# Instruction order of every engine from a list scheduler at build time, in a channel attention and highway network kernel

## The chip, the cores and the metric

The kernel runs on one core of a Trainium2 chip. The metric is the device time of one execution in microseconds (us). Every run that is quoted was taken as fast (undisturbed). A profiled run's span, from its first to its last instruction, is about 1.8 us shorter than its time (349.39 against 347.5 us, 307.13 against 305.3 us). Runs of one call share a chip and the runs of the kernel before; different calls ran on different chips, so across calls I compare ratios or stretches of a profile.

## The reference

There are four batches of N = 6336 tokens with C = 256 channels. The attention is over channels: the score matrix is only 256 x 256 per batch, but it is a sum over all tokens. A gated layer follows.

```python
qn = q / (np.linalg.norm(q, axis=1, keepdims=True) + 1e-06)   # over the tokens
kn = k / (np.linalg.norm(k, axis=1, keepdims=True) + 1e-06)
s = kn.transpose(0, 2, 1) @ qn / tau                          # 256 x 256 for each batch
a = softmax(s)                                                # over the last axis
x = v @ a
H = relu(x @ w_h);  T = sigmoid(x @ w_t + b_t)
out = T * H + (1 - T) * x
```

## The kernel before

Each batch has three parts, and they depend on each other in this order.

- **Stage 1**: 50 steps of six matmuls on TensorE (PE) that sum k·q and the two Gram matrices, whose diagonals are the squared norms, in one accumulator `sg`.
- **The chain**: from `sg` to the attention matrix. VectorE (DVE) takes the diagonals and computes roots and reciprocals in some 20 tiny operations, each needing the one before; PE spreads the result over the partitions (`cqb`); then come scale, exp on ScalarE (ACT), row sums, four transposes on PE (`atps`) and a fold with the layer's weights (`ah`). Almost nothing of it is work; it is latency.
- **Stage 2**: 25 pairs of row blocks (100 in the whole program). For each, PE transposes v (`vtps`), multiplies (`xh`) and computes the gate (`t`); ACT does a relu and the gate's function; DVE does a difference and, for every second pair, a product and the result.

Stage 2 of a batch is mixed with stage 1 of the next. The order was written by hand: `due` tells how many stage-1 steps should be done after a pair, and one step of the chain is taken after each pair. Every engine executes in the order in which instructions are written: the timeline in the prediction shows PE standing 5.79 us before `cqb`, with the next pair written behind it.

```python
LOOK = 2
ENDS = [17, 42, 69]          # the pairs at which stage 1 of batches 1, 2, 3 ends
...
    def chain(b):
        ...
        first = [diagonals, guess, refine, root, bcast]        # bcast holds the matmul cqb
        if b == B - 1:
            return [lambda: [f() for f in first], exps, soft, trans, fold]
        return [diagonals, lambda: (guess(), refine()), lambda: (root(), bcast()),
                exps, soft, trans, fold]
...
        if end:                                                # the last batch
            eng = nc.gpsimd if i % 4 == 1 and not single else nc.vector
            eng.tensor_tensor(out=dd[...], in0=uu[...], in1=dd[...], op=AluOp.mult)
...
            xh, tt = main(b, i)                                # PE: the pair
            got = elementwise(b, i, xh, tt, pending)           # ACT and DVE
            ...
            want = due(g)
            if steps:
                steps.pop(0)()                                 # one step of the chain
            while s1 < want:                                   # stage-1 steps of the next batch
                stage1(1 + s1 // NS, s1 % NS)
                s1 += 1
                if s1 % NS == 0:
                    steps = chain(s1 // NS)
                    steps.pop(0)()
```

## Time and profile before

| | before |
|---|---|
| time, median of 3 runs | 349.55 us (349.28 to 349.7) |
| span of the profiled run | 347.5 us |
| PE busy | 288.6 us, 83% |
| DVE, ACT, GpSimd busy | 59%, 51%, 18% |
| mean granted PE clock | 0.944 |

The page's rows of busy tenths cut the span into 40 slices; a nine means 90% or more. The view that I use most, though, is the start of each pair's `xh` matmuls in the timeline. A pair costs PE 1.74 us and a stage-1 step 0.44; where two pairs start further apart than the work between them, PE has stood still or run at half clock. The prediction shows the slices, the stretches and the timeline.

### The profile page before, as it was taken

Reading aid. Unit: us, or ns where it says so; the run is one execution under the profiler, and the core shown is the slowest. Engines: PE = TensorE matmul, PEld = TensorE weight load, DVE = VectorE, ACT = ScalarE, POOL = GpSimd, SP = SyncE. Lnnn points to the kernel's source line nnn. Section 1 sums busy time; section 2 is a strip of 40 time slices with the busy share of each in tenths; the row PEclk is TensorE's granted clock in tenths of the full one; section 3 lists DMA queues with packets and bytes.
Section 4 is the critical chain, followed back from the end, with each engine's and each line's share of the span. In section 5 each row is a group of like instructions: output and inputs, shape, how many; then the busy total and the mean of one; then the engine's idle time right before and its main releaser. Section 6 shows DMA issues by size and latency. Waiting matters only on the chain.

```text
span 347.5 us, 6183 instructions
## 1 busy us (share of the span) xinstructions
PE 288.6 (83%) x2540; PEld 207.1 (60%) x2540; DVE 206.0 (59%) x331; ACT 177.8 (51%) x322; POOL 63.1 (18%) x102
## 2 busy tenths in 40 slices
PE   0969699999995789999995789999993786888883
PEld 0858567777773467777763467776772354555541
DVE  1000235666675377677686277777677385777775
ACT  1000246666561355665672365666662378777762
POOL 6214422212111212211111000000010002222220
PEclk9998989999998799999999799999997699999995
DMA  7999999999999999999999963466643203222233
GB/s 132 213 213 211 209 214 213 222 265 271 269 245 244 234 251 247 248 270 271 250 252 258 232 146 143 75 170 181 173 144 61 121 1 145 121 121 123 121 124 143
DMA packets 16828, 65.54 MB, mean 189 GB/s; under 512 B 1952, under 2 KB 3616, under 8 KB 13856
## 3 DMA queue, kind: packets, MB, share of 16 engines
q0 software_dynamic: 12608, 39.20, 58.1%
q1 hardware_dynamic: 4192, 25.95, 18.6%
q8 instruction: 20, 0.33, 0.3%
q14 instruction: 8, 0.07, 0.1%
HBM read 78.38 MB, written 25.95 MB: 300 GB/s over the span
## 4 chain that ended last, share of the span: by engine, by line
PE 56%; DVE 17%; DMA 8%; issue 6%; ACT 5%; POOL 4%; POOLq 1%; ACTq 0%; DVEq 0%
PE xh L398 19%; PE sg L191 9%; PE t L408 8%; DVE o L473 6%; PE vtps L381 5%; DMA q<-in_q_dram 5%; PE sg L193 5%; PE sg L192 5%; DVE dd L438 4%; PE t L405 4%; POOL dd L449 3%; DMA k<-in_k_dram 3%; ACT hh L431 3%; DVE dd L453 1%; DVE junk L213 1%
## 5 line engine op out<-in xcount | busy, mean ns | idle before, releaser
L438 DVE TENSOR_TENSOR dd<-hh,xh 128x512 f32<-128x512 f32 (+1 forms) x100 | 68.7, 687 | 81.5 <-ACT hh L431 80.9
L431 ACT ACTIVATE hh<-xh 128x512 f32<-128x512 f32 (+1 forms) x100 | 59.7, 597 | 100.3 <-PE xh L398 57.1
L398 PE MATMUL xh<-mr,vtsb 128*128 128x512 f16 (+1 forms) x400 | 108.0, 394 | 2.0 <-DVE vtsb L386 2.0
L191 PE MATMUL sg<-q,k 128*128 128x256 f16 x384 | 95.4, 286 | 14.3 <-DMA k<-in_k_dram 13.3
L193 PE MATMUL sg<-q 128*128 128x128 f16 x384 | 87.4, 228 | 0.0
L192 PE MATMUL sg<-k 128*128 128x128 f16 x384 | 87.4, 227 | 0.0
L432 ACT ACTIVATE uu<-t 128x512 f32<-128x512 f32 (+1 forms) x100 | 59.7, 597 | 7.7 <-PE t L408 2.2
L473 DVE SCALAR_TENSOR_TENSOR o<-dd,hh 128x1024 f32<-128x1024 f32 (+1 forms) x49 | 58.7, 1198 | 4.9 <-POOL dd L449 4.9
L408 PE MATMUL t<-mr,vtsb 128*128 128x256 f16 (+1 forms) x400 | 61.2, 276 | 0.0
L384 ACT COPY vtsb<-vtps 128x512 f16<-128x512 f16 (+1 forms) x93 | 53.6, 577 | 13.3 <-PE vtps L381 13.3
L408 PEld LDWEIGHTS <-vtsb 128*128 128x128 f16 (+1 forms) x400 | 40.3, 101 | 29.1 <-issue 4.6
L398 PEld LDWEIGHTS <-vtsb 128*128 128x128 f16 (+1 forms) x400 | 36.7, 102 | 28.3 <-issue 3.8
L381 PE MATMUL vtps<-ident,v 128*128 128x128 f16 x384 | 37.5, 221 | 15.3 <-DVE gs L294 7.4
L453 DVE SCALAR_TENSOR_TENSOR dd<-uu,dd 128x1024 f32<-128x1024 f32 (+1 forms) x39 | 46.2, 1184 | 4.4 <-ACT uu L432 0.9
L191 PEld LDWEIGHTS <-k 128*128 128x128 f16 x384 | 39.3, 102 | 15.5 <-DMA k<-in_k_dram 13.8
L193 PEld LDWEIGHTS <-q 128*128 128x128 f16 x384 | 39.4, 103 | 6.1
L381 PEld LDWEIGHTS <-v 128*128 128x128 f16 x384 | 29.8, 99 | 19.3 <-issue 17.0
L405 PE MATMUL t<-btb,row 128*128 128x512 f16 (+1 forms) x100 | 39.0, 390 | 1.7 <-ACT uu L432 1.7
L192 PEld LDWEIGHTS <-k 128*128 128x128 f16 x384 | 39.4, 103 | 0.9 <-issue 0.5
L80 POOL DMA_DIRECT2D v<-in_v_dram x24 | 12.8, 533 | 109.0 <-PE vtps L381 71.6
L213 DVE SCALAR_TENSOR_TENSOR junk<-sg,ident 128x128 f32<-128x128 f32 x16 | 4.6, 290 | 36.1 <-ACT gs L209 35.7
L449 POOL TENSOR_TENSOR dd<-uu,dd 128x1024 f32<-128x1024 f32 x6 | 14.2, 2361 | 65.1 <-DVE dd L438 65.1
(63 smaller groups left out, 130.6 us busy)
## 6 DMA issues: line engine op xcount, KB each, us to landing
out_dram<-o SPq DMA_DIRECT2D x23, 1024.0 KB, 4.6
v<-in_v_dram POOLq DMA_DIRECT2D x24, 512.0 KB, 19.2
q<-in_q_dram POOLq DMA_DIRECT2D x23, 512.0 KB, 20.2
k<-in_k_dram POOLq DMA_DIRECT2D x23, 512.0 KB, 20.2
out_dram<-ot SPq DMA_DIRECT2D x4, 192.0 KB, 2.6
q<-in_q_dram POOLq DMA_DIRECT2D x2, 256.0 KB, 14.5
k<-in_k_dram POOLq DMA_DIRECT2D x2, 256.0 KB, 11.2
out_dram<-o SPq DMA_DIRECT2D x1, 512.0 KB, 2.7
```

The lines of the kernel that those rows point to most:

```text
L191: nc.tensor.matmul(sg[:, c, 0:C], ka[:, cs], qa, start=first, stop=False)
L192: nc.tensor.matmul(sg[:, c, C : C + P], ka[:, cs], ka[:, cs], start=False, stop=False)
L193: nc.tensor.matmul(sg[:, c, C + P : C + 2 * P], qa[:, cs], qa[:, cs], start=False, stop=last)
L381: nc.tensor.transpose(ps[:, u, c, 0:nr], src[:, bass.ts(c, P)], ident[0:nr, 0:nr])
L384: eng.copy(out=vt[:, :, :, 0:nr], in_=ps[:, :, :, 0:nr])
L398: nc.tensor.matmul(xh[0:nr, u, :], vt[:, u, kt, 0:nr], mr[kt][:, 0 : 2 * C], start=(kt == 0), stop=(kt == 1),)
L405: nc.tensor.matmul(tt[0:nr, :, :], row0[:, 0:nr], btb, start=True, stop=False)
L408: nc.tensor.matmul(tt[0:nr, u, :], vt[:, u, kt, 0:nr], mr[kt][:, 2 * C : 3 * C], start=False, stop=(kt == 1 and u == 0),)
L431: nc.scalar.activation(out=hh[0:nr, us, :], in_=xh[0:nr, :, C : 2 * C], func=Act.Relu)
L432: nc.scalar.activation(out=uu[0:nr, us, :], in_=tt[0:nr, :, :], func=Act.Sigmoid if end else Act.Tanh, scale=-1.0 if end else -0.5,)
L438: nc.vector.tensor_tensor(out=dd[0:nr, us, :], in0=hh[0:nr, us, :], in1=xh[0:nr, :, 0:C], op=AluOp.subtract)
L473: nc.vector.scalar_tensor_tensor(out=ot, in0=dd[0:nr, us, :], scalar=-1.0 if end else -0.5, in1=hh[0:nr, us, :], op0=AluOp.mult, op1=AluOp ...
```

## The change

All arithmetic becomes tasks. A task knows its engine, a key (smaller is sooner), how long it occupies the engine (`pitch`), how long until its result can be used (`lat`), what it depends on, and which buffers it takes and frees. At build time a simulation picks, whenever an engine is free, the ready task with the smallest key. Loads and stores run through a model of the DMA (a common rate, a lag, at most eight loads under way). The simulated order is then emitted as the program. The chain's tasks have key -50, so they go before everything that is ready.

```diff
-LOOK = 2
-ENDS = [17, 42, 69]
+ENDS = [16, 41, 68]
+class Plan:
+    RATE = 422e3
+    LAG = 1.8
+    LANES = 8
...
+        def ready(x):
+            return (
+                not x.left
+                and x.at <= t + eps
+                and all(self.rings[g].open_at(t + eps) for g in x.take)
+                and (x.eng != "POOL" or not x.size or sum(d > t + eps for d in lanes) < self.LANES)
+            )
...
+            return min(
+                (x for x in avail[e] if ready(x)), key=lambda x: (x.key, x.n), default=None
+            )
...
+        def several(fns, x):                   # a row of tiny DVE operations as one task
+            d = 0.2 * len(fns)
+            return dve(lambda: [f() for f in fns], d - 0.06, d, [x])
...
+        cqb = x = pe(bcast, 0.85, [x], take=["vt"])
...
+        ready[b] = plan_chain(b, first, x, -50)
...
+            xh[i] = plan.add(
+                "PE", g, 0.86, 1.06, [ev[i]] + ready[b], lambda i=i: main_xh(b, i), take=["xh"]
+            )
...
-            if steps:
-                steps.pop(0)()
-            while s1 < want:
-                stage1(1 + s1 // NS, s1 % NS)
...
-            eng = nc.gpsimd if i % 4 == 1 and not single else nc.vector
...
+    nc.scalar.preload_act_table(Act.Sqrt)
+    for x in plan.run():
+        if x.fn is not None:
+            x.fn()
```

Besides the order, some things change in kind: the last batch uses tanh like the others and no longer gives every fourth product to GpSimd; all copies of transposed v go to ACT; several copies of the chain move from DVE to ACT in batches 1 to 3; and in batch 0 the table for the root is loaded at the start, that for exp directly after the root.

## The prediction

> **What bounds the kernel now.** I read the busy table of the page first (PE 288.6 us, 83% of the span; DVE 59%; ACT 51%), then the slices, then busy time by stretches of 20 us. A share over the whole span hides that there are several stages, so the stretches decide. First PE's row of the slices, in tenths:
>
> ```profile
> PE   0969699999995789999995789999993786888883
> ```
>
> Then the stretches. Columns: stretch; its length; busy us of PE, PEld, DVE, ACT, POOL; granted clock; DMA share; GB/s.
>
> ```profile
> 20.00:40.00 20.00, 16.26 (x195) 14.61 (x192) 0.26 (x2) 0.86 (x2) 6.21 (x11) 0.91 1.10 209
> ...
> 80.00:100.00 20.00, 20.00 (x200) 15.15 (x199) 13.24 (x15) 12.09 (x23) 3.71 (x7) 1.00 1.06 264
> 100.00:120.00 20.00, 12.98 (x93) 8.44 (x91) 11.64 (x35) 7.58 (x16) 4.23 (x8) 0.86 1.06 240
> ...
> 180.00:200.00 20.00, 12.71 (x82) 8.28 (x81) 10.81 (x34) 6.68 (x14) 1.58 (x3) 0.83 1.06 249
> ...
> 240.00:260.00 20.00, 20.00 (x193) 14.83 (x192) 14.40 (x17) 13.23 (x24) 1.57 (x3) 1.00 0.56 155
> 260.00:280.00 20.00, 11.70 (x66) 6.70 (x64) 11.25 (x36) 7.44 (x17) 0.00 (x0) 0.74 0.31 84
> ...
> 300.00:320.00 20.00, 17.16 (x126) 10.62 (x125) 14.06 (x18) 14.91 (x27) 7.09 (x3) 1.00 0.38 155
> ```
>
> The reader is to see four stages. Until 39 us PE waits for q and k of batch 0 (DMA full). From 51 us PE is full, with three holes near 110, 190 and 270 us: there the softmax chains of batches 1 to 3 run. From 285 us, when no q, k work (stage 1) is left, PE is no longer full.
>
> Next I took the start of each of the 100 row pairs (the groups of four L398 matmuls in the timeline). In the full stretches the spacing is 2.62 us with two stage-1 steps between, 2.18 with one, 3.06 with three, 1.74 with none: so a pair costs PE 1.74 us and a step 0.44, without exception. Every spacing above that is lost time:
> - chain 1, pairs 18 to 23: 29.2 us where 6 x 2.62 = 15.7 are due. 13.5 over, of which the chain's own matmuls are 1.9 (0.85 + 0.22 + 0.86). Lost: 11.6.
> - chain 2, pairs 43 to 48: 28.9 against 15.3. Lost: 11.7.
> - chain 3, pairs 69 to 73: 24.2 against 9.6. Lost: 12.7.
> - last stage: pairs 76, 78, 82, 86, 90, 94 take 3.3 to 3.6 each instead of 1.74. Lost: 9.9. Pair 98 takes 3.71: lost 2.0.
>
> Sum 47.9 us of the 347.5 us span. The timeline shows why for chain 3:
>
> ```profile
> 262.63 0.59 ACT L209 COPY gs<-sg 128x512 f32<-128x512 f32 x1
> 263.44 0.28 DVE L213 SCALAR_TENSOR_TENSOR junk<-sg,ident 128x128 f32<-128x128 f32 x1
> ...
> 268.39 1.19 PE L288 MATMUL cqb<-dcat,ones 128*128 128x256 f32 x2 [5.79 <-DVE dcat L279]
> ...
> 269.37 1.91 PE L398 MATMUL xh<-mr,vtsb 128*128 128x512 f16 x4
> ...
> 271.37 0.60 ACT L431 ACTIVATE hh<-xh 128x512 f32<-128x512 f32 x1 [8.15 <-PE xh L398]
> ```
>
> The order written by hand puts the broadcast matmul cqb right behind the last stage-1 step. PE is in order, so it stands 5.8 us while VectorE does some 20 tiny dependent operations (about 0.2 us each, 0.16 busy), and the next pair then runs at half clock. In the last stage the idle of PE is due to one thing in each four pairs: a product given to GpSimd, on which VectorE and then PE wait; it takes 2361 ns there, and the same product takes 1225 ns on VectorE (groups by form):
>
> ```profile
> L453 DVE SCALAR_TENSOR_TENSOR dd<-uu,dd 128x1024 f32<-128x1024 f32 x36 | 44.1, 1225 | 4.4 <-ACT uu L432 0.9
> ...
> L449 POOL TENSOR_TENSOR dd<-uu,dd 128x1024 f32<-128x1024 f32 x6 | 14.2, 2361 | 65.1 <-DVE dd L438 65.1
> ```
>
> **What the Trainium skill says.** "TensorE: Matmul & The Clock Gate", part 1 (What's actually happening), says the array falls to half clock after about 3.4 us of idleness and needs about 3.4 us of work to return. The trace agrees: after the holes four matmuls of 512 take 1.91 us instead of 1.03, and a stage-1 step 0.85 instead of 0.44 from 42.96 to 45.94 us; a hole of 2.2 us (ending at 24.85 us) was enough too. So a hidden hole gives back its length and some 1.7 us more (half of 3.4; an estimate). "ScalarE: Activation LUTs", What ACT_TABLE_LOAD costs, gives about 1283 ns for a table load; the page here has four of 1283 ns, and § Table sets puts exp and tanh in one set, which the trace confirms (no load between them). "Perfetto Trace Analysis", Optimizing Scalar/DVE Operations, says that profiled latency exceeds engine time because the write's end overlaps with the next instruction. The trace agrees: 128x512 on VectorE lasts 0.69 but the next starts 0.60 later; 128x1024 lasts 1.22 and gives way after 1.14; ACT 0.60 against 0.50.
>
> **The change part by part.** The arithmetic is nearly the same: 5070 rows on PE in both programs. I read the changed program's order on each engine.
>
> 1. Chains 1 and 2. Between the last stage-1 step and cqb, PE now has 2 pairs less a little, 2 transposes and 6 steps of the next batch: 2 x 0.86 + 2 x 0.64 + 2 to 3 x 0.22 + 6 x 0.44 = 6.2 us. VectorE needs for the same: 4 diagonals 1.34, one 0.60 difference, 17 small ones 3.4, and a wait of up to 1.14 for a running operation: about 6. From cqb to the transposes of the softmax, PE has 4.5 us (2 pairs' products, 3 steps) against scale 0.75 behind up to 2.3 of VectorE work, exp 1.3, reciprocal 0.35, two scalings 0.7: some 5. I allow 1.5 us of loss per chain: gain 10.1 + 10.2.
>
> 2. Chain 3 has no next batch to fill with. Up to cqb PE has 3 xh (2.58), 2 t (1.28) and 5 transposes (1.1): 5.0 us, but the 2 buffers of xh make pairs 70 and 71 wait for differences that stand in VectorE's order behind the diagonals and behind the small ones. Walking the order by hand, the first pair of batch 3 starts some 17 to 18 us after the last step, with about 12.5 us of PE work in it. I take 5.5 us lost: gain 7.2.
>
> 3. Chain 0. The sqrt table is loaded at the start and the exp table behind the root; the copy of sg moves behind the diagonals. The chain's inputs come 0.6 (copy) and 1.28 (table) earlier. But PE's order now has all 8 steps and a transpose before the softmax transposes, and after 2.8 us of idleness they would run at half clock: 4 x 0.85 + 4 x 0.44 + 0.2 = 5.4 us after cqb, about the time of before (8 of before's were also there). Gain 0.5, at most 2.
>
> 4. Last stage, 25 pairs. GpSimd's 6 products of 2.36 return to VectorE, sigmoid becomes tanh (one table load of 1.28 less, at 288 us). VectorE per two pairs: 2 x 0.60 + 2 x 1.14 = 3.48, plus about 0.12 where the product waits for the difference just before it, so 1.80 a pair; PE needs 1.74; ACT 3 x 0.50. The stage is thus bound by VectorE and PE almost equally. Gain 9.9 less 25 x 0.08 = 2: 7.9.
>
> 5. The end. The copy of the last transposed pair goes back to ACT without waiting: of 2.0 us I count 1.5 and 1.0 for the last pair, now at full clock. Gain 2.5.
>
> Sum 0.5 + 10.1 + 10.2 + 7.2 + 7.9 + 2.5 = 38.4. Span 347.5 - 38.4 = 309.1; the timed runs are 2.05 above the span (349.55), so **311 us**.
>
> **Rivals.** (a) The transfers become the bound. For: the DMA share is above 1 until 200 us. A load of 1.05 MB is issued every 2.46 us, 426 GB/s. "DMA: Bandwidth & Descriptors", Where 436 GB/s comes from, gives about 435 as the ceiling, so there is no more to be had. Against: up to the end of stage 1 of batch 1 some 35 such units (q, k of two batches 25, v 6, outputs 4) are due, 3 + 86 = 89 us, and PE is there at 97 at best; for batch 3 it is about 213 against some 238. The margin is 8 us in the first phase, and late tiles would cost there: time 316 to 322. (b) The static order is wrong on the chip: a scheduler that takes a wait for 0.5 us too short puts an instruction in front that blocks an in-order engine. For: chain 3's cqb stands behind pair 71. Every chain losing 4 us more would give 323. (c) VectorE bounds more than the last stage, because it took over GpSimd's work; at 1.95 a pair the stage gains 4 us less: 315. (d) All chains hide completely, also chain 3: 311 - 3 - 4 = 304.
>
> **Range and chances.** Costs I can't see are likelier than gains: 304 to 321. To lose the 2% (7 us), four fifths of the gain would have to vanish, though 48 us of idle PE are really there: faster 0.97, within 2% 0.02, slower 0.01.
>
> **What would show it.** Spacing of pairs near 18 to 24 and 43 to 49 close to 1.74 + 0.44 per step; no idle of PE before cqb above 1.5 us for chains 1 and 2; clock 1.0 in those stretches; stage 1 of batch 3 over near 238 us; a spacing of 1.8 in the last stage and VectorE 95% busy there; PE waits for DMA only before 39 us. New DMA waits at 50 to 100 us, or half clock in the chains, would make it wrong.

## More of the kernel before

One more view of the kernel before: PE's waits, by what it waited for. Columns: total us, number of waits, longest.

```profile
PE cqb L288 <- DVE dcat L279: 17.4, 4, 5.8
PE sg L191 <- DMA k<-in_k_dram: 13.3, 4, 9.2
PE vtps L381 <- DVE gs L294: 7.4, 3, 2.6
PE vtps L381 <- DVE vtsb L386: 7.2, 5, 1.5
```

The reader is to see that the first and third row are the chain, at two different places; the fourth is the last stage, where PE waits for a copy of transposed v on DVE. The second is the start, in which PE waits for the first q and k.

## The result and the profile after

| | before | after |
|---|---|---|
| time, median of 4 runs | 349.41 us (346.51 to 349.7) | 307.86 us (307.13 to 308.78) |
| span of the profiled run | 347.5 us | 305.3 us |
| PE busy | 288.6 us, 83% | 274.8 us, 90% |
| DVE busy | 206.0 us, 59% | 204.6 us, 67% |
| mean granted PE clock | 0.944 | 0.996 |

The ratio is 0.883 (95% interval 0.877 to 0.888). A ratio here is the mean time of one kernel's fast runs over the mean of the other's fast runs of the same rounds, so not quite the ratio of the medians. The output is correct in this and in every run below.

PE's slices and clock in the page after, in tenths:

```profile
PE   0886867999999999999999999999999789999981
...
PEclk9999999999999999999999999999999999999998
```

Of the three holes one shallow dip is left, and the last quarter is full. The stretches of the kernel after (columns as in the prediction):

```profile
100.00:120.00 20.00, 20.00 (x193) 15.04 (x192) 16.65 (x34) 13.85 (x29) 3.69 (x7) 1.00 1.05 264
160.00:180.00 20.00, 19.56 (x178) 13.96 (x176) 17.73 (x45) 13.79 (x29) 3.69 (x7) 1.00 1.06 254
...
240.00:260.00 20.00, 16.67 (x118) 10.20 (x116) 18.31 (x32) 15.94 (x33) 0.00 (x0) 1.00 0.29 116
260.00:280.00 20.00, 19.98 (x149) 12.41 (x147) 19.37 (x23) 17.83 (x35) 0.00 (x0) 1.00 0.29 119
280.00:300.00 20.00, 17.50 (x120) 10.25 (x118) 19.44 (x24) 15.12 (x29) 0.00 (x0) 1.00 0.46 185
```

The first two stretches hold chains 1 and 2: PE is full, where before it had 12.98 of 20 us near 110. The third holds chain 3. The last two are the last stage: DVE is 97% busy and PE keeps up with it until the work runs out near 299 us. PE's waits of the kernel after:

```profile
PE sg L354 <- DMA k<-in_k_dram: 13.9, 5, 8.9
PE cqb L512 <- DVE dcat L500: 2.6, 1, 2.6
PE t L653 <- ACT uu L684: 2.5, 2, 1.3
PE xh L641 <- ACT mr L601: 1.6, 2, 1.2
```

The wait at `cqb` has become one of 2.6 us instead of four with 17.4; it is chain 0's, for which there is no stage 2 to fill with. The DMA wait is the start, as before; after 45 us PE waits for no DMA at all. By the starts of the pairs, the span divides like this (us; "lost" is what exceeds the PE work between those pairs at full clock, with the chain's own matmuls taken as work):

| part | before | after | gain |
|---|---|---|---|
| start to the first pair | 50.87 | 49.38 | 1.5 |
| chain 1, lost | 11.6 | 0.15 | 11.5 |
| chain 2, lost | 11.7 | 0.6 | 11.1 |
| chain 3, lost | 12.7 | 4.8 | 7.9 |
| last stage (pairs 75 to 98), lost | 9.9 | 1.2 | 8.7 |
| from pair 98 to the end | 11.9 | 11.3 | 0.6 |
| the chains' own matmuls, now at full clock | 3 x 1.93 | 3 x 1.57 | 1.1 |

The gains sum to 42.4 us, and the spans differ by 42.2. As an example of the working: after the change pairs 18 to 24 start within 20.47 us after pair 17; seven pairs at 1.74, 15 steps at 0.4375 and 1.57 us of chain matmuls make 20.31, so 0.15 us are lost.

### The profile page after: what moved, and what is told of

Read it like the earlier page. It is cut to its first block, busy times and chain, and to the rows that moved or that the text cites. A ratio compares the mean times of both kernels' runs of the same rounds, so it can differ in the third digit from the quotient of the medians.

```text
span 305.3 us, 6171 instructions
## 1 busy us (share of the span) xinstructions
PE 274.8 (90%) x2540; PEld 200.0 (66%) x2540; DVE 204.6 (67%) x321; ACT 178.5 (58%) x336; POOL 48.7 (16%) x96
## 4 chain that ended last, share of the span: by engine, by line
PE 63%; DVE 18%; DMA 9%; issue 3%; ACT 3%; POOL 1%; ACTq 0%; DVEq 0%; POOLq 0%
PE xh L641 20%; PE sg L354 11%; PE t L656 10%; PE sg L355 6%; PE sg L356 6%; DMA q<-in_q_dram 6%; DVE o L722 6%; DVE dd L693 5%; PE vtps L628 5%; PE t L653 5%; DVE dd L703 5%; DMA k<-in_k_dram 4%; PE ah L590 1%; DVE junk L391 1%; ACT hh L676 1%
## 5 line engine op out<-in xcount | busy, mean ns | idle before, releaser
L354 PE MATMUL sg<-q,k 128*128 128x256 f16 x384 | 93.0, 276 | 14.6 <-DMA k<-in_k_dram 13.9
L641 PE MATMUL xh<-mr,vtsb 128*128 128x512 f16 (+1 forms) x400 | 102.7, 379 | 2.7 <-ACT mr L601 1.6
L355 PE MATMUL sg<-k 128*128 128x128 f16 x384 | 85.1, 222 | 0.0
L356 PE MATMUL sg<-q 128*128 128x128 f16 x384 | 85.1, 222 | 0.0
L703 DVE SCALAR_TENSOR_TENSOR dd<-uu,dd 128x1024 f32<-128x1024 f32 (+2 forms) x53 | 61.6, 1163 | 14.3 <-ACT uu L684 12.9
L656 PE MATMUL t<-mr,vtsb 128*128 128x256 f16 (+1 forms) x400 | 60.0, 273 | 0.0
L634 ACT COPY vtsb<-vtps 128x512 f16<-128x512 f16 (+1 forms) x100 | 57.7, 577 | 2.3 <-PE vtps L628 2.2
L354 PEld LDWEIGHTS <-k 128*128 128x128 f16 x384 | 38.0, 99 | 21.2 <-DMA k<-in_k_dram 14.6
L355 PEld LDWEIGHTS <-k 128*128 128x128 f16 x384 | 38.1, 99 | 7.7 <-issue 1.1
L356 PEld LDWEIGHTS <-q 128*128 128x128 f16 x384 | 38.0, 99 | 4.8
L653 PE MATMUL t<-btb,row 128*128 128x512 f16 (+1 forms) x100 | 37.9, 379 | 2.5 <-ACT uu L684 2.5
## 6 DMA issues: line engine op xcount, KB each, us to landing
q<-in_q_dram POOLq DMA_DIRECT2D x2, 256.0 KB, 14.6
k<-in_k_dram POOLq DMA_DIRECT2D x2, 256.0 KB, 11.3
```

The lines of the kernel that those rows point to most:

```text
L354: nc.tensor.matmul(sg[:, c, 0:C], ka[:, cs], qa, start=first, stop=False)
L355: nc.tensor.matmul(sg[:, c, C : C + P], ka[:, cs], ka[:, cs], start=False, stop=False)
L356: nc.tensor.matmul(sg[:, c, C + P : C + 2 * P], qa[:, cs], qa[:, cs], start=False, stop=last)
L634: nc.scalar.copy(out=vt[:, :, :, 0:nr], in_=vt_ps.pop((b, i))[:, :, :, 0:nr])
L641: nc.tensor.matmul(xh[0:nr, u, :], vt[:, u, kt, 0:nr], mr[kt][:, 0 : 2 * C], start=(kt == 0), stop=(kt == 1),)
L656: nc.tensor.matmul(tt[0:nr, u, :], vt[:, u, kt, 0:nr], mr[kt][:, 2 * C : 3 * C], start=False, stop=(kt == 1 and u == 0),)
```

## The experiments

My theory: the gain is that of PE's idle time, in two independent pieces. Each chain is a row of waits on an engine that executes in order, and the scheduler puts other PE work between its steps; in the last stage PE no longer waits for DVE, which stood behind GpSimd. Four rivals:

- **One instruction**: a single badly placed one per chain (`cqb`) causes the whole loss, and no scheduler is needed.
- **Urgency** makes the gain.
- **Transfers** are the next bound, and the DMA model is what keeps the order right.
- **Any scheduler** would do; its durations need not be precise.

Where an expectation names theories by letters, the letters belong to that text alone. In the timeline lines below, the columns are the start, the duration, engine, line and operation, output and inputs, and in brackets the idle time before it and what ended that.

### The last stage alone (on the kernel before)

```diff
-            func=Act.Sigmoid if end else Act.Tanh,
-            scale=-1.0 if end else -0.5,
+            func=Act.Tanh,
+            scale=-0.5,
...
-            eng = nc.gpsimd if i % 4 == 1 and not single else nc.vector
...
-                on_dve = b == B - 1 and i % 4 == 2
-                transposes(n // NP, n % NP, nc.vector if on_dve else nc.scalar)
+                transposes(n // NP, n % NP, nc.scalar)
```

> The kernel before, with only the last batch changed as the new kernel has it: products on VectorE instead of GpSimd, tanh instead of sigmoid, all transposed pairs copied by ACT. My theory: the GpSimd product is what makes pairs 76 to 94 take 3.3 us each now and then, so the last stage gains about 8 us and the three chains stay as they are: 341 us (339 to 343), spacing 1.74 to 1.85 us in the last stage. Rival (the GpSimd product is not the cause, the hand-made order is): under 3 us gained, 346 to 349.

Measured: 340.81 us (338.16 to 341.54) against 349.25, ratio 0.976 (0.970 to 0.981): a gain clear of noise, though not surely one of 2%. The chains still lose 12.4, 11.7 and 12.4 us, and pairs from 77 on are 1.74 us apart, later 1.74 and 1.92 in turn. The stretch of this kernel that lies wholly in the last stage:

```profile
300.00:320.00 20.00, 19.93 (x146) 12.34 (x145) 19.48 (x23) 18.59 (x35) 0.00 (x0) 1.00 0.34 138
```

PE went from 17.16 (as the prediction shows it) to 19.93 of 20 us, with the same DVE rate as in the scheduled kernel. So 8.4 us of the 42 have nothing to do with the scheduler: moving six products from GpSimd to DVE, the gate and the copies by hand gives them. The edit makes these three changes at once, and no run takes them apart. The trace of the kernel before shows what PE stood for once in four pairs:

```profile
302.93 1.23 DVE L473 SCALAR_TENSOR_TENSOR o<-dd,hh 128x1024 f32<-128x1024 f32 x1 [0.80 <-POOL dd L449]
304.07 0.42 DVE L386 COPY vtsb<-vtps 128x512 f16<-128x512 f16 x1
304.54 0.38 PE L381 MATMUL vtps<-ident,v 128*128 128x128 f16 x4 [1.42 <-DVE vtsb L386]
```

DVE stood 0.80 us for GpSimd's product, then did the result `o` in 1.23 us, and only then the copy for which PE waited. So the place of that copy in DVE's order is a rival cause beside GpSimd: moving the copies to ACT alone might have given much of the gain. That was not run.

### `cqb` one pair further behind its inputs, by hand (on the kernel before)

```diff
-        return [diagonals, lambda: (guess(), refine()), lambda: (root(), bcast()),
+        return [diagonals, lambda: (guess(), refine(), root(), bcast()), cast,
                 exps, soft, trans, fold]
```

Here `cast` holds only the matmul `cqb`. In chains 1 and 2 it keeps its place on PE, and the tiny operations go to DVE one pair earlier; in chain 3 `cqb` comes one pair later; chain 0 stays.

> The kernel before, with the chain's tiny VectorE operations put one pair ahead of the broadcast matmul: for chains 1 and 2 PE's order does not change at all, for chain 3 the matmul stands one pair later. Theory A (the hole is only PE standing in front of the broadcast matmul): of the 12 us lost per chain some 4 to 6 us come back each (4.2 us of waiting and up to 1.7 us of half clock), 333 to 338 us. Theory B (each step of the chain makes PE wait in its own place, and a wait removed turns up at the next, as the transposes that wait for the PSUM bank the broadcast holds): under 2 us each, 344 to 349.

Measured: 342.06 us (340.52 to 343.32), ratio 0.981 (0.976 to 0.986): some 7 us gained, clear of noise, though not surely 2%. PE's waits in this kernel:

```profile
PE cqb L291 <- DVE dcat L279: 12.0, 4, 4.0
PE vtps L384 <- DVE gs L297: 7.5, 3, 2.6
```

The wait at `cqb` fell from 17.4 to 12.0; the next wait of the chain is as it was (7.4 before). Losses were 9.7, 8.3 and 11.7 in the three chains (11.6, 11.7, 12.7 before; in the last of them over pairs 69 to 74). The gain lies between what the two theories expected. One pair's work covers only a part of the wait at `cqb`, and nothing of the waits after it: a chain stalls PE at every place where its steps meet PE, and each must be covered. By hand this means placing `cqb`, the transposes and the fold of each chain among the pairs. The rival of the one instruction explains 7 of some 30 us.

### The chain without urgency

```diff
-        ready[b] = plan_chain(b, first, x, -50)
+        ready[b] = plan_chain(b, first, x, -50 if b == 0 else NP * b - 0.5)
```

Now a chain's task counts as much as the first pair that needs it.

> The new kernel with one number changed: the chains of batches 1 to 3 have the priority of the first pair that needs them, instead of a priority ahead of everything. If urgency carries the gain in the holes, PE runs out of pairs at each batch boundary: 3 to 8 us lost per chain, 317 to 330 us, and the VectorE-bound stretches behind each boundary show pairs without stage-1 steps between. If any order without blocking does it (the scheduler, not the urgency), within 1%: 305 to 311.

Measured: 316.88 us (316.11 to 319.02), ratio 0.910: about 9 us slower than the change. But where? The profiled run is the slowest of the four; its span is 11.9 us longer. The first pair came at 51.83 us (49.38 after), so 2.4 us are the start, which the edit does not touch. Pair 74 came only 1.4 us later than in the kernel after, so chains 1 and 2 cost nothing, although pairs 24 and 25 are now 11.42 us apart: PE fills the time with 17 steps of the next batch. Chain 3 has no next batch. From pair 74 to pair 75 it takes 10.23 us instead of 3.95, 6.3 us more. The stretch of chain 3 without urgency:

```profile
240.00:260.00 20.00, 13.49 (x89) 7.77 (x87) 16.35 (x42) 13.15 (x28) 0.00 (x0) 0.89 0.36 128
```

PE has 13.49 us busy at a clock of 0.89, against 16.67 at 1.00 with urgency. The other 4.1 us lie in the last stage: pairs 75 to 98 take 45.3 us instead of 41.2, and every fourth of them 2.48. There PE waits 0.51 us for a difference that stands behind a result in DVE's order; why the scheduler arrives at this order is left open.

### Urgent only in chains 0 and 3

```diff
+        ready[b] = plan_chain(b, first, x, NP * b - 0.5 if 0 < b < B - 1 else -50)
```

> The new kernel with chains 1 and 2 at ordinary priority and only chain 3 urgent. If urgency pays only where PE has no stage-1 step left to fill with (chain 3), 307 to 309. If chains 1 and 2 carry their part of the 9 us that e3 lost, 310 to 314.

Measured: 308.98 us (308.23 to 309.75), ratio 0.887; the kernel after, run again, had 308.77 and 0.887. So urgency is worth nothing in chains 1 and 2, and its whole value lies in the chain that has no filler and in the last stage behind it. The rival of urgency holds for that one chain.

### The same without a DMA model

```diff
-    RATE = 422e3
-    LAG = 1.8
+    RATE = 422e9
+    LAG = 0.0
```

Transfers take almost no time in the build-time simulation; the chip's transfers are what they were.

> The new kernel with the scheduler believing that transfers take no time. PE's order then differs from the new kernel's only in the first 60 tasks around chain 0: three transposes of v and two stage-1 steps stand before the broadcast matmul of chain 0, and v of batch 0 lands only at about 44 us. My theory: the DMA model matters only there, 3 to 6 us lost: 311 to 314. Rival: the transfers' model is what keeps PE from waiting all along: over 10 us lost, with waits of PE on DMA after 60 us.

Measured: 313.85 us (313.67 to 314.73), ratio 0.901, 6 us slower than the change. The timeline of this kernel around chain 0:

```profile
38.71 0.22 PE L356 MATMUL sg<-q_t 96*128 96x128 f16 x1
44.36 0.61 PE L628 MATMUL vtps<-ident,v 128*128 128x128 f16 x4 [5.44 <-DMA v<-in_v_dram]
45.65 0.59 PE L628 MATMUL vtps<-ident,v 128*128 128x128 f16 x4 [0.67 <-ACT vtsb L634]
...
50.57 1.16 PE L512 MATMUL cqb<-dcat,ones 128*128 128x256 f32 x2
```

The scheduler believed that v was there and put its transposes ahead of `cqb`; PE, in order, stood 5.44 us for the transfer, then ran at half clock. The first pair began at 59.48 instead of 49.38 us. Seven further stage-1 steps had been done by then, 3.1 us of work, and the rest stayed lost (pair 17 came 6.6 us later). After 60 us the two orders are alike and no DMA is waited for. So the DMA model is worth 6 us, all of them at one spot at the start.

### Tiny DVE operations held for four times too short

```diff
-            d = 0.2 * len(fns)
+            d = 0.05 * len(fns)
```

> The new kernel with the scheduler told that each of the chain's tiny VectorE operations takes 0.05 us instead of 0.20 (they measure 0.20). The broadcast matmul is then put 1 to 2 pairs too early in PE's order. My theory: an in-order PE pays for a duration that is told too short, 1.5 to 2.5 us for each of chains 1 to 3: 312 to 316, with waits of PE for the dcat operations of 1 us or more at those chains. Rival (the order is forgiving, PE catches up elsewhere): within 1 us, 307 to 309.

Measured: 316.12 us (315.85 to 316.58), ratio 0.906: 8.3 us slower. One row of PE's waits tells it:

```profile
PE cqb L512 <- DVE dcat L500: 9.2, 4, 2.6
```

Four waits instead of one, 9.2 us instead of 2.6. From the first pair to the end it takes 263.3 us instead of 255.9: 7.4 us more, for three more waits of 2.2 us. The scheduler put `cqb` where it thought its input ready, so PE stopped there, exactly as with the order by hand. So not any scheduler would do: durations four times too short bring the waits back. How close they must be was not tested.

### More to transfer: 8 or 24 further loads

Between the loads of batch 1 on, loads of 0.52 MB of v into a buffer that nobody reads:

```diff
+        if n % 6 == 2 and n < 48:              # 8 loads; 24 with n % 2 == 0
+            plan.add("POOL", len(plan.tasks), 0.54, 0, [], lambda n=n: load_more(n), size=...)
```

> The new kernel with 8 further loads of 0.52 MB that nobody uses, spread over batches 0 to 2 (8 x 1.23 us = 9.8 us of transfer at the measured 426 GB/s). If transfers are near the bound but not it (the margin of my prediction: 8 us in the first phase, of which these take 3.7), at most 2 us more: 307 to 310. If transfers already set the pace, all of it: 317 to 318.

> The same with 24 further loads, 29.5 us of transfer. With a margin of 8 us in the first phase and 10 to 20 later, the excess shows: 9 to 20 us more, 317 to 327, and waits of PE for DMA behind 60 us. If transfers set the pace already, 29 us more: 337. If there were no bound near, 308.

Measured with 8: 308.89 us (308.46 to 309.87), ratio 0.886. From the first pair to the end 256.0 us, against 255.9 in the kernel after, though 9.8 us of transfer (8 x 0.52 MB at 426 GB/s) are added; the 1 us in the total is the start. With 24: 320.71 us (320.45 to 320.81), ratio 0.919; 268.0 us from the first pair, 12.1 more for 29.5 us of transfer added. I had expected PE's waits to name the DMA in that case. They hardly do (0.8 us after 60 us), because the scheduler knows of the slower loads and moves the work: stage-1 steps come in lumps, and in such stretches the pairs are 0.86, 7.04, 1.76 and 1.74 us apart in turn. GpSimd, which issues the loads, also waited for the two spare buffers, so that this run slowed the issue as well as the transfers. The transfers are thus not the bound at the size of the case: they have a margin of some 10 us at least, and where between 10 and 30 us it ends is open.

### A third `hh` buffer

The end gained less than I had predicted (0.6 against 2.5 us). The timeline of the kernel after shows ACT waiting for DVE there, because a new pair's relu needs a `hh` buffer that a result has yet to free:

```profile
297.08 0.60 ACT L676 ACTIVATE hh<-xh 128x512 f32<-128x512 f32 x1 [2.19 <-DVE o L722]
...
298.22 0.38 PE L653 MATMUL t<-btb,row 128*96 128x512 f16 x1 [1.31 <-ACT uu L684]
```

```diff
-        "hh": 2,
+        "hh": 3,
```

> The new kernel with a third hh buffer. At the end the relu of pair 98 waits 2.2 us for an hh buffer and the last pair's t for 1.3 us. If that wait sets the end, about 1 us less: a ratio of 0.997. If VectorE's backlog sets the end anyway, within 0.2 us.

Measured: 306.9 us (305.48 to 307.45), ratio 0.879 (0.876 to 0.882); from the first pair to the end 254.45 us, 1.5 less than 255.92. The spacing in the last stage becomes 1.74, 1.74, 1.73, 1.83, PE's wait for `uu` falls from 2.5 to 0.7 us. So the buffer caused much of the alternation between 1.74 and 1.92. Of the 1.5 us, 0.8 lie between pairs 75 and 98, 0.4 in chain 3 and only 0.4 after pair 98: it was a small part of the end's loss.

### The kernel after again, and with PE kept busy in chain 0

The runs of the kernel after fall into two groups: 307.13 and 307.38 us at a clock of 0.996, 308.33 and 308.78 at 0.980. The suspicion: the 2.56 us hole before chain 0's `cqb` sometimes halves the clock. The test puts 38 small matmuls, whose result nobody reads, into it:

```diff
+            def warm():
+                wt = new("vt", [P, P], f32, "warm")
+                for _ in range(38):
+                    nc.tensor.matmul(wt, ident, ident, start=True, stop=True)
+            x_w = pe(warm, 2.2, [last, consts], take=["vt"])
```

> The new kernel once more, unchanged, so that the next ones are compared on the same chip: 307 to 309, with runs of a lower clock share (0.98) about 1 us above those at 0.996.

> The new kernel with 38 small matmuls of no use in the 2.6 us in which PE waits for the broadcast of chain 0. If the 1 to 3 us by which the first pair starts later in some runs (49.4 to 52.1 us) come from half clock after that wait, every run now starts it near 49.4 and the times fall together at 307.0 to 307.5, clock 0.99. If it comes from something else (arrival of q and k), the spread stays, 307 to 309.

Measured: 308.77 us (308.37 to 309.12) for the kernel after, 307.37 (307.06 to 307.41) with the small matmuls; six runs each, and all six of the second lie below all six of the first. The stretch just after `cqb`, first of the kernel after, then with the small matmuls:

```profile
43.00:46.00 3.00, 3.00 (x24) 2.54 (x23) 1.27 (x5) 1.09 (x4) 1.41 (x3) 0.51 1.07 214
```

```profile
43.00:46.00 3.00, 3.00 (x45) 2.85 (x43) 1.19 (x5) 1.62 (x5) 1.29 (x3) 1.00 1.05 212
```

Both say "PE busy 3.00 of 3.00", but the first does half as many matmuls, at a granted clock of 0.51. In the kernel after's own profile the same stretch had 1.00 with the same hole of 2.56 us: the clock is halved after it in one run and not in another, and what decides that is not shown. The whole difference of the two profiled runs of this call lies before the first pair (51.30 against 49.60 us; from there 255.97 and 255.98). With the hole filled all six runs are at 0.987 to 0.996. The mean clock alone does not tell the groups apart, though: two runs of the kernel after had 0.987 and 0.990 and still took 308.89 and 308.37 us.

### The two together

Three `hh` buffers, the small matmuls and `ENDS = [15, 42, 68]`.

> Third hh buffer, the small matmuls, and stage 1 of batch 2 stretched by one pair (ends 15, 42, 68): 1.5 us from the buffer, 0.7 from the clock, about 0.5 from the ends: 305.0 (304 to 306.5).

Measured: 305.28 us (305.18 to 305.41, six runs), ratio 0.877 (0.873 to 0.880). It beats both kernels; against the kernel after in the same call it is 3.5 us faster. No run takes the new `ENDS` apart from the other two.

## Why the prediction was right

The prediction was 311 us with a range of 304 to 321; 307.86 us were measured. Every part of its sum can be read off the table of the result.

- **The chains.** Predicted gains 10.1, 10.2 and 7.2, measured 11.5, 11.1 and 7.9. I had allowed 1.5 us of loss for chains 1 and 2; only 0.15 and 0.6 remain, and of the 5.5 allowed for chain 3, 4.8. For it the detail was right too: from the last step to the first pair of batch 3 it takes 17.5 us (17 to 18 predicted), and the timeline after shows pair 71 and `cqb` where the order had them:

```profile
242.23 1.02 PE L641 MATMUL xh<-mr,vtsb 128*128 128x512 f16 x4 [0.30 <-DVE dd L693]
243.09 0.59 PE L512 MATMUL cqb<-dcat,ones 128*128 128x256 f32 x2
```

- **The last stage.** Predicted 7.9, measured 8.7, with DVE at 97%; done alone it gave 8.4 us. The prediction put the idle time down to "one thing", GpSimd's product. That is not shown: the copies on DVE, changed with it, stand in the same wait. The sum also has a slip: 1.80 less 1.74 is 0.06 a pair, not 0.08.
- **The clock.** The prediction counted the half clock after each hole; in the stretches of chains 1 to 3 the clock is now 1.00. Its reading that a hole of 2.2 us halves the clock holds only at times: that hole is 2.06 us in the trace, and one of 2.13 us in the kernel after, ending at 24.52, is followed by full clock. The full clock adds about 1.1 us for the chains' own matmuls, which I had left out of the sum.
- **The start.** I predicted 0.5, counting on half clock after the hole; the profiled run gained 1.5 because the clock held. In the repeated run it did not, and the first pair came at 51.30 us, 0.4 later than before. So 0.5 lies between the two cases; the 1.5 of the profiled run was luck.
- **The end: mis-sized.** The step "of 2.0 us I count 1.5 and 1.0 for the last pair" gave 2.5, and 0.6 was measured. The 1.5 came true: from pair 98 to pair 99 it takes 1.93 us instead of 3.71. The 1.0 failed: from pair 99 to the end it takes 9.5 us instead of 8.2. I had counted PE's clock there. In fact DVE, almost saturated through the whole last stage, arrives with a backlog: from 293.2 us to its last result at 302.2 it is never idle for more than 0.11 us. The third `hh` buffer gave 0.4 us here and left DVE as full, so the backlog is what remains.
- **The rivals.** (a) Late transfers did not appear, and 10 us more of them cost nothing. (b) A wrong static order does cost what the rival feared, in its order of size: 8.3 us when durations were falsified, against 12 reckoned at 4 us per chain. It did not occur because the durations were close. (c) 1.95 us per pair did not occur: 1.79 on average. For (a) the prediction sets 426 GB/s beside a ceiling of 435 that the page gives for the SBUF side; but 426 is what is read from HBM, and half of it lands (1.05 MB of f32 become the 512 KB of f16 that the page of the run lists). What the trace shows is that the DMA engines are full (share 1.06 to 1.10).

Five terms were too low by 0.7 to 1.4 us, the left-out one added 1.1 and one was too high by 1.9. The sum of the gains was therefore 4.0 us too low (42.4 against 38.4); it is luck that the 1.9 cancelled a part of the other 5.9. Two figures of the prediction don't come out of the record: the 2.05 us between span and time set a median against the profiled run's span (the profiled runs have 1.9 and 1.8), and the "5070 rows on PE" stand in no view; the pages count 2540 matmuls and 2540 weight loads in both kernels.

What stays open: the 4.8 us that chain 3 still loses (the order there was read, but no run takes its parts apart), the 2.48 us of every fourth pair without urgency, which of the three changes of the last stage matters, and the exact margin of the transfers. Nor does any run keep the order by hand and move only the chain's copies from DVE to ACT. In each chain they take 1.46 us on DVE before and 1.69 us on ACT after, little beside the 11.1 and 11.5 us gained in chains 1 and 2.

## What to carry to other kernels

Measure a hole as the spacing between equal pieces of work minus the work in between; that told 47.9 us of loss here, of which about 41 came back. A chain of small dependent operations stalls an in-order engine at each place where it touches it, so put independent work ahead of every one of these instructions: covering a part of the first left the next wait untouched. A scheduler at build time did this well here with measured durations, and lost 8.3 us when one of them was told four times too short. In this kernel urgency paid only where no filler work exists, and the transfer model only where data are really late.

## What the Trainium skill lacked or had wrong

- "TensorE: Matmul & The Clock Gate", Why this matters for your kernels, advises against idle gaps of more than some 3 us between bursts of matmuls. Here a gap of 2.56 us halved the clock in some runs (0.51 from 43 to 46 us) and not in others (1.00), and filling it took the times from 308.77 to 307.37 us. The hole of 2.06 us (ending at 24.85 us) in the kernel before was followed by half clock too. So the limit is too generous for these runs; the page derives it from one idle window, of about 3.4 us, and all these holes are shorter than that.
- "DMA: Bandwidth & Descriptors", Where 436 GB/s comes from, has the HBM side at about 358 GB/s as what binds transfers from HBM to SBUF, and that sentence lacks its condition: earlier, under its measurements, the page says that this is the rate with both cores of a pair streaming. Here, on one core, loads that read 1.05 MB each from HBM went through every 2.46 us, which is 426 GB/s read.
- "ScalarE: Activation LUTs", What ACT_TABLE_LOAD costs, adds about 1380 ns of draining to the load's 1283 ns. The load is 1.28 us here, but the drain is not seen: in the kernel after the root ends at 40.33 us, the load starts at 40.36 and the next ACT instruction at 41.65, 0.01 us after its end: 1.32 us in all for the switch of sets.
